# Attention and two mixture layers in one kernel: w2 and the result moved in 4 KB packets, the first blocks of w_in loaded first, products grouped by tiling

## The chip, the cores and the metric

One core of a Trainium2 chip. Its engines are TensorE (PE in the rows, PEld for its weight loads), VectorE (DVE), ScalarE (ACT), GpSimd (POOL) and SyncE (SP), which here issues all DMAs. The metric is the device time of one execution in microseconds, the median of the runs.

## The reference

Attention with a forgetting bias, a layer of squared ReLU, and a soft mixture of 8 experts, one after the other, over 2304 tokens of width 512:

```python
scores = scale * q @ k.T            # 4 batches, 8 heads, 576 positions, head_dim 64
cum = cumsum(maximum(s, 0))
scores = where(causal, -1e9, scores + minimum(-(cum[:, None] - cum[None, :]), 0))
x = softmax(scores) @ v             # heads side by side: 2304 x 512
x = maximum(x @ w_in, 0) ** 2 @ w_out          # 512 -> 2048 -> 512
logits = x @ phi                    # 32 slots: 8 experts x 4
slot_input = softmax(logits, axis=0).T @ x
for e in range(8):
    slot_out[e] = maximum(slot_input[e] @ w1[e], 0) @ w2[e]    # w1 512x1024, w2 1024x512
out = softmax(logits, axis=1) @ slot_out
```

## The kernel before, in words

Every piece of work is a task: a function that issues instructions, with its buffers, a priority and a planned cost for each engine that can do it. `Plan.add` (line 222) makes a task, `Plan.run` (line 248) simulates the five engines with these costs and writes the program out in the order in which it places the tasks. At each step it looks, engine by engine, for the earliest start and takes the first task by priority that can start within WAIT = 100 ns of it (line 303). `FACTOR` scales the planned costs of an engine, `prio` shifts the priority of what is added inside it, and STEP is 1000 priority steps' worth of one stage. The order on every engine, SP's DMAs included, is what this planner made of the numbers.

Attention works on 16 pairs of heads (a batch and two heads) and tiles of 128 query rows. A score tile is a run of products with 64 partitions by 128 columns of weights (L660 q times k in two f16 parts, L663 the causal mask, L665 the bias), the two heads on the two halves of TensorE's rows. The softmax's probabilities, written by L691, are transposed by DMA (L732) and multiplied with v in L791, with 128 by 64 weights. The rows of 128 tokens, as two f16 parts, go into L833: 4 column blocks of w_in (512 columns each) times 12 products with 128 by 128 weights, in two units of 6. The relu and the square (L848 and after) follow; L873 transposes, L890 multiplies with w_out times phi (128 by 32 weights), L918 to L952 keep the running softmax over tokens and add up slot_input in the basis of the 2048 columns. The MoE tiles start once their four pairs are done, so that attention and L833 alternate on TensorE for most of the time. The form of the weights, 64x128, 64x64, 128x64, 128x32, 32x128 or 128x128, is called the tiling below.

w_in and w_out come as 64-bit numbers and are converted to f32 by ACT, DVE and POOL (`f64_load`, `f64_convert`, L496 to L501), then split into f16 parts (L426 and L432 among them; `scaled` can put L426 on ACT, DVE or POOL). `conv_steps` (L1027) keeps up to 6 blocks of 512 KB loading ahead. The forgetting bias starts from s: 8 DMAs (L1043 to L1046) bring it in, each with 16 partitions; L1054 and L1055 make the cumulative sum, and L1059 to L1062 three bf16 rows of it (`cum3`), which L665 needs.

The tail of the kernel begins at L1240. L1249 multiplies with w_out, L1257 transposes, and for each expert `hidden` (L1270, L1276) makes the 1024 hidden values of all 32 slots from w1, and `project` (L1289) multiplies with half of w2's columns and adds into one PSUM bank for each half, `so`. After the last expert `combine(0)` spreads the sum (L1297), splits it into two bf16 parts (L1298 to L1301) and makes 18 tiles of the result (L1308 and L1309), whose columns 0 to 255 are written; then the experts' second halves and `combine(1)` follow for columns 256 to 511. w1 and w2 are loaded in units of 512 KB (`w_unit`, L1172; `w1_load`, L1195, 4 KB in one run of memory; `w2_load`, L1199, 128 partitions by 4 rows by 256 columns, that is 1 KB runs). The loads of all experts' w1 and first halves of w2 come first, the second halves of all last. The result of two tiles goes out as 128 partitions by 2 rows by 256 columns, 256 KB in 1 KB runs; every fifth tile straddles two batches and goes out alone as 2 by 64 rows by 256 columns.

Of the kernel before, what the change touches and what calls it, by code (L numbers as in the profile page):

```python
# [22 lines left out]
N_QK = 2  # L23
Q_AT = 8
# [19 lines left out]
N_OB = 6  # L44
# [41 lines left out]
FACTOR = {"P": 1.0, "V": 1.15, "A": 1.1, "G": 1.3, "D": 1}  # L86
# [112 lines left out]
class Task:  # L199
    def __init__(self, alts, prio):  # L200
        self.alts, self.prio, self.deps, self.succ, self.bufs, self.end, self.gap = alts, prio, set(), [], [], None, 0


class Plan:
# [134 lines left out]
def attention_moe_softmoe(ctx, tc, qk, v, s, w_in, w_out, w_out_t, phi, w1, w2, cst, out):  # L339
# [191 lines left out]
    def wout_conv(raw, c, kd):  # L531
# [108 lines left out]
    def a_scores(P, i):  # L640
# [15 lines left out]
        if i < 4:  # L656
# [9 lines left out]
            add([*qk, sel, mask, cum3, rows_h], pss, P=((5 if plain(P) else 4) * (10 + n / 2.4) + 200, mul))  # L666
            for h, ps in enumerate(pss):
                add([ps], [(m, 2 + h)], V=(60 + 1.04 * n, lambda ps=ps, h=h: nc.vector.reduce_max(out=m.t[:, 2 + h:3 + h], in_=ps.t[:, 0:n], axis=AX.X)))  # L668
        else:
            for ps, c0, c1 in ((pss[0], 0, 512), (pss[1], 512, 576)):  # L670
# [83 lines left out]
    def a_pv(P, i):  # L754
# [17 lines left out]
        else:  # L772
# [12 lines left out]
            ns = (54 if i < 4 else 46) * len(mms) + 90  # L785
# [6 lines left out]
        add(vv + [pt], [x], P=(ns, mul))  # L792
# [31 lines left out]
    def m_h(t, c):  # L824
# [557 lines left out]
```

## Time and profile before

| what | us |
|---|---|
| median of 3 runs | 574.12 |
| lowest, highest | 570.63, 576.21 |
| the profiled execution, its own time | 577.03 |
| its span, from first to last instruction | 575.3 |
| TensorE busy | 503.0 (87%) |
| VectorE busy | 375.3 (65%) |
| ScalarE busy | 329.2 (57%) |
| GpSimd busy | 191.3 (33%) |
| mean granted clock of TensorE | 0.961 of full speed |
| memory read and written | 77.85 MB, 4.72 MB |

The rows further down are of the profiled execution. Times count from the start of its span; "idle before" is the idle time of the engine just before an instruction, with what ended it.

### The profile page before, as it was taken

What the parts mean: (1) busy time and instruction counts of PE and PEld (TensorE: products, weight loads), DVE (VectorE), ACT (ScalarE), POOL (GpSimd) and SP (SyncE); (2) the same over time, 40 slices, a digit from 0 to 9 for tenths busy, and PEclk for the clock granted to TensorE, in tenths of its full rate; (3) what the DMA queues carried; (4) which work ended last, traced back from release to release, by engine and by line L of the source; (5) the groups of instructions that cost most, each with busy time, mean ns of one, the idle gap of its engine ahead of it and who ended that gap; (6) DMA issues with size and microseconds to landing.
All of it is one profiled execution on the core that took longest, in us unless ns stands there. A gap on an engine that the chain in (4) does not pass through costs nothing.

```text
span 575.3 us, 13522 instructions
## 1 busy us (share of the span) xinstructions
PE 503.0 (87%) x5151; PEld 279.2 (49%) x5153; DVE 375.3 (65%) x977; ACT 329.2 (57%) x820; POOL 191.3 (33%) x319
## 2 busy tenths in 40 slices
PE   1268789989999999999999999999989989799771
PEld 1134446556455565554655555555544544345341
DVE  4777988988997988899898766776454231301210
ACT  2866886877776576775665565654555644311132
POOL 3735854662641733363452223311222100000100
PEclk9996789999999999999999999999998999999976
DMA  7986755244555654874664224442888995499985
GB/s 235 385 283 205 254 154 182 86 148 102 127 136 108 131 126 60 139 159 102 127 116 66 52 56 84 79 96 51 232 273 285 322 329 183 155 361 370 349 268 165
DMA packets 122761, 102.72 MB, mean 179 GB/s; under 512 B 81096, under 2 KB 102216, under 8 KB 122696
## 3 DMA queue, kind: packets, MB, share of 16 engines
q1 hardware_dynamic: 122696, 101.86, 62.8%
q8 instruction: 40, 0.66, 0.5%
q14 instruction: 25, 0.20, 0.1%
HBM read 77.85 MB, written 4.72 MB: 144 GB/s over the span
## 4 chain that ended last, share of the span: by engine, by line
PE 61%; DVE 18%; DMA 7%; ACT 4%; issue 3%; POOL 3%; SPq 1%; ACTq 0%; DVEq 0%; POOLq 0%
PE bank L833 26%; DVE sbuf L432 7%; PE bank L791 5%; PE bank L873 5%; PE bank L660 4%; DVE sbuf L668 3%; PE bank L952 3%; PE bank L1270 3%; PE bank L890 2%; DVE sbuf L425 2%; DMA out_dram<-sbuf 2%; POOL sbuf L426 2%; PE bank L675 2%; PE bank L1289 2%; DMA sbuf<-in_w_dram 2%
## 5 line engine op out<-in xcount | busy, mean ns | idle before, releaser
L833 PE MATMUL bank<-sbuf 128*128 128x512 f16 x864 | 206.2, 382 | 2.1 <-DVE sbuf L432 1.4
L833 PEld LDWEIGHTS <-sbuf 128*128 128x128 f16 x864 | 79.4, 98 | 89.7 <-issue 6.7
L443 ACT COPY sbuf<-bank 128x512 f32<-128x512 f32 (+6 forms) x139 | 63.2, 470 | 102.6 <-PE bank L873 37.8
L691 ACT ACTIVATE sbuf<-bank,sbuf 128x512 f32<-128x512 f32 (+4 forms) x160 | 93.1, 586 | 38.8 <-DVE sbuf L685 36.4
L432 DVE SCALAR_TENSOR_TENSOR sbuf<-sbuf 128x512 f16<-128x512 f32 (+5 forms) x149 | 100.8, 703 | 2.6 <-POOL sbuf L426 1.6
L426 POOL TENSOR_SCALAR sbuf<-sbuf 128x512 f16<-128x512 f32 (+9 forms) x97 | 73.6, 764 | 61.8 <-DVE sbuf L714 26.9
L668 DVE TENSOR_REDUCE sbuf<-bank 128x1 f32<-128x128 f32 (+3 forms) x128 | 58.2, 480 | 5.8 <-PE bank L665 5.4
L713 POOL TENSOR_SCALAR sbuf<-sbuf 128x2 f32<-128x2 f32 (+1 forms) x74 | 17.8, 240 | 132.0 <-ACT sbuf L691 92.7
L791 PE MATMUL bank<-sbuf 128*64 128x128 f16 (+4 forms) x1296 | 57.0, 228 | 1.1 <-DMA sbuf<-sbuf 0.6
L444 DVE COPY sbuf<-bank 128x512 f32<-128x512 f32 (+5 forms) x55 | 28.0, 513 | 43.2 <-PE bank L873 18.8
L848 ACT ACTIVATE sbuf<-bank,sbuf 128x512 f32<-128x512 f32 x53 | 36.4, 688 | 34.3 <-PE bank L833 33.6
L499 POOL TENSOR_SCALAR sbuf<-sbuf 128x512 int32<-128x512 uint8 x46 | 34.7, 755 | 61.3 <-DMA sbuf<-in_w_out_dram 32.9
L660 PE MATMUL bank<-sbuf 64*128 64x128 f16 (+7 forms) x352 | 46.2, 363 | 9.2 <-DMA sbuf<-in_qk_dram 8.9
L873 PE MATMUL bank<-sbuf 128*128 128x128 f32 x288 | 44.7, 278 | 1.7 <-ACT sbuf L443 1.2
L501 DVE SCALAR_TENSOR_TENSOR sbuf<-sbuf 128x512 int32<-128x512 int32 x48 | 35.2, 740 | 16.6 <-ACT sbuf L496 9.4
L449 ACT ACTIVATE sbuf<-sbuf 128x512 bf16<-128x512 f32 (+1 forms) x60 | 39.1, 652 | 8.8 <-DMA sbuf<-in_v_dram 4.3
L873 PEld LDWEIGHTS bank<-sbuf 128*128 128x128 f32 x288 | 34.1, 143 | 17.0 <-ACT sbuf L443 2.2
L496 ACT ACTIVATE sbuf<-sbuf 128x512 f32<-128x512 f32 x48 | 31.1, 663 | 17.8 <-DMA sbuf<-in_w_in_dram 10.4
L791 PEld LDWEIGHTS <-sbuf 128*64 128x64 f16 (+1 forms) x1056 | 28.7, 110 | 17.8 <-issue 16.6
L851 ACT ACTIVATE sbuf<-sbuf 128x512 f32<-128x512 f32 x50 | 31.5, 629 | 8.6 <-DVE sbuf L849 7.6
L425 DVE TENSOR_SCALAR sbuf<-sbuf 128x512 f16<-128x512 f32 (+8 forms) x71 | 34.5, 492 | 1.8 <-DMA sbuf<-in_v_dram 0.5
L744 PE MATMUL bank<-sbuf 128*128 128x128 f32 (+1 forms) x100 | 19.4, 313 | 16.9 <-POOL sbuf L426 12.7
(140 smaller groups left out, 675.0 us busy)
## 6 DMA issues: line engine op xcount, KB each, us to landing
sbuf<-in_w_dram SPq DMA_DIRECT2D x48, 512.0 KB, 8.8
sbuf<-in_qk_dram SPq DMA_DIRECT2D x16, 576.0 KB, 5.1
sbuf<-in_w_in_dram SPq DMA_DIRECT2D x16, 512.0 KB, 7.9
sbuf<-in_w_out_t_dram SPq DMA_DIRECT2D x16, 512.0 KB, 4.1
sbuf<-in_w_out_dram SPq DMA_DIRECT2D x16, 512.0 KB, 4.7
sbuf<-in_w_dram SPq DMA_DIRECT2D x32, 256.0 KB, 5.4
sbuf<-in_v_dram SPq DMA_DIRECT2D x28, 256.0 KB, 3.5
out_dram<-sbuf SPq DMA_DIRECT2D x16, 256.0 KB, 5.1
```

The lines of the kernel that those rows point to most:

```text
L425: "V": (130 + 0.52 * n, lambda: nc.vector.tensor_scalar(out=out_(), in0=in_(), scalar1=scale(), scalar2=None, op0=ALU.mult)),
L426: "G": (244 + 0.834 * n, lambda: nc.gpsimd.tensor_scalar(out=out_(), in0=in_(), scalar1=scale(), scalar2=1.0, op0=ALU.mult, op1=ALU.mult)),
L432: alts = {"V": (base + 1.04 * n, lambda: nc.vector.scalar_tensor_tensor(out=out_(), in0=in_(), scalar=scale(), in1=hi(), op0=ALU.mult, op1 ...
L443: "A": (51 + 0.834 * n, lambda: nc.scalar.copy(out=out_(), in_=in_())),
L449: add(r + [junk], w, A=(186 + 0.834 * n, lambda: nc.scalar.activation(out=junk.t[:, 0:n], in_=in_(), func=AF.Abs, accum_out=acc_())))
L660: nc.tensor.matmul(ps.t[:, 0:n], q_(D[h], slice(128 * i, 128 * i + 128)), k_(D[h], slice(0, n)), start=j == 0, stop=False)
L668: add([ps], [(m, 2 + h)], V=(60 + 1.04 * n, lambda ps=ps, h=h: nc.vector.reduce_max(out=m.t[:, 2 + h:3 + h], in_=ps.t[:, 0:n], axis=AX.X)))
L691: ex = lambda t, o, n, ps, h, k: add([nm, sc, ps], [t, (sums, k)], A=(373 + 0.834 * n, lambda: nc.scalar.activation(out=t.t[:, o:o + n], i ...
L791: nc.tensor.matmul(x.t[64 * h:64 * h + 64, c0:c1], lhs, rhs, start=n == 0, stop=n == len(mms) - 1)
L833: nc.tensor.matmul(ps.t, X.t[:, e, kd, :], w[c].t[:, kd, :], start=kd == 0 and e == 0 and w is wh, stop=kd == KD - 1 and e == 1)
L848: add([ps, (sc, b)], [g], A=(571, lambda: nc.scalar.activation(out=g.t, in_=ps.t, func=AF.Relu, scale=sc.t[:, b, c:c + 1])), V=(630, lambd ...
L873: nc.tensor.transpose(ps.t[:, j * 128:(j + 1) * 128], g.t[:, j * 128:(j + 1) * 128], ident)
```

## The change

It has six parts.

1. w2 is loaded with two consecutive rows per partition (`(p k) f -> p (k f)`, k = 2), all 512 columns: 4 KB runs in units of 512 KB (two 2 KB runs in the first, halved units). `hidden` transposes strided columns so that the hidden values stand in the matching order. Each expert's w1 and w2 are loaded one after the other.
2. `project` works on all 512 columns at once, in one bank; `combine` runs once, for two halves of the columns up to `sst`, and its products go into banks of 512 columns. The result goes out as two consecutive rows per partition (4 KB runs, 512 KB), and a tile that straddles two batches as two DMAs of 64 partitions by 2 KB.
3. The first two blocks of w_in are issued right after the constants, ahead of s and qk; later blocks get a priority that is 30 steps back.
4. s comes in two DMAs of 64 partitions, whose DRAM side reads the 16 rows of a head parity 4 times (outermost dimension 4 with step 0), in place of 8 DMAs of 16.
5. The planner: each TensorE task has a tiling; among the tasks that can start within 100 ns of the earliest, one with the tiling of the product before is preferred, if its priority is at most 6 STEPs behind, and 95 ns are planned for a change of tiling. The planned costs of TensorE's tasks are edited throughout.
6. FACTOR of ACT 1.1 to 1.15, of POOL 1.3 to 1.05; DMA's planned cost 1.2 to 1.08; N_OB 6 to 5 (with buffers of twice the size), h1_p 2 to 3 buffers.

```diff
-FACTOR = {"P": 1.0, "V": 1.15, "A": 1.1, "G": 1.3, "D": 1}
+FACTOR = {"P": 1.0, "V": 1.15, "A": 1.15, "G": 1.05, "D": 1}
...
-                        best = first, e, next((s, t) for s, t in options if s <= first + WAIT)
+                        options = [(s, t) for s, t in options if s <= first + WAIT]
+                        if e == "P":
+                            prio = options[0][1].prio + SAME * STEP
+                            options.sort(key=lambda o: o[1].tiling != tiling or o[1].prio > prio)
+                        best = first, e, options[0]
...
+            if e == "P":
+                ns += 0 if task.tiling == tiling else 95
+                tiling = task.tiling
...
-        add(vv + [pt], [x], P=(ns, mul))
+        add(vv + [pt], [x], P=(ns, mul), tiling=(128, 64))
...
-                    raw[j] = blocks[j][0](*blocks[j][2:])
+                    with prio(0.03 if j >= N_AT_ONCE else 0):
+                        raw[j] = blocks[j][0](*blocks[j][2:])
...
+    next(conv)
+    dma(410, lambda: cs.t, lambda: cst, [], [cs])
     for h in range(2):
-        for e in range(4):
-            o = 64 * h + 16 * e
-            dma(60, lambda o=o: s_sb.t[o:o + 16], lambda h=h: bass.AP(tensor=s.tensor, offset=s.offset + h * S, ap=[[2 * S, B * NP], [1, S]]), [], [(s_sb, o)])
-    dma(410, lambda: cs.t, lambda: cst, [], [cs])
+        dma(240, lambda h=h: s_sb.t[64 * h:64 * h + 64], lambda h=h: bass.AP(tensor=s.tensor, offset=s.offset + h * S, ap=[[0, 4], [2 * S, B * NP], [1, S]]), [], [(s_sb, h)])
     qk_load(pairs[0])
-    with prio(5):
-        next(conv)
...
-    def w2_load(e, hf):
-
-        src = w2[e, :, hf * HD:(hf + 1) * HD].rearrange("(a k p) f -> a p k f", k=4, p=128)
-        wt[e, 1, hf] = w_unit(src[0], []) + w_unit(src[1], [])
+    def w2_load(e):
+
+        wt[e, 1] = [u for g in range(4) for u in w_unit(w2[e, 256 * g:256 * g + 256, :].rearrange("(p k) f -> p (k f)", k=2), [])]
...
-                nc.tensor.transpose(ph.t[:, c * 128:(c + 1) * 128], h1.t[:, c * 128:(c + 1) * 128], ident)
+                nc.tensor.transpose(ph.t[:, c * 128:(c + 1) * 128], h1.t.rearrange("p (q c) -> p c q", c=2)[:, c], ident)
...
-                    w = a2[2 * a + g // 2][1]()[:, g % 2 * HD:(g % 2 + 1) * HD]
-                    nc.tensor.matmul(so.t[32 * g:32 * g + 32, 0:HD], z.t[:, 4 * a + g, :], w, start=e == 0 and a == 0, stop=e == E - 1 and a == 1)
+                    nc.tensor.matmul(so.t[32 * g:32 * g + 32, :], z.t[:, 4 * a + g, :], views[4 * a + g][1](), start=e == 0 and a == 0, stop=e == E - 1 and a == 1)
...
-                rows = out[row:row + 128 * n, hf * HD:(hf + 1) * HD].rearrange("(a p) d -> p a d", p=128)
-                dma(365 * n, lambda rows=rows: rows, lambda n=n, o_=o_: o_.t[:, 0:n * HD].rearrange("p (a d) -> p a d", a=n), [o_], [])
+                dma(1500, lambda row=row, n=n: out[row:row + 128 * n, :].rearrange("(p k) d -> p (k d)", k=n), lambda o_=o_: o_.t.rearrange("p k d -> p (k d)"), [o_], [])
             else:
-                rows = out.rearrange("(b r) d -> b r d", r=S)[b0:b + 1, S - 64:S, hf * HD:(hf + 1) * HD]
-                dma(365, lambda rows=rows: rows, lambda o_=o_: o_.t[:, 0:HD], [o_], [])
+                for j, q_ in enumerate((b0, b)):
+                    dma(370, lambda q_=q_: out[q_ * S + S - 64:q_ * S + S, :], lambda j=j, o_=o_: o_.t[64 * j:64 * j + 64, 0, :], [o_], [])
...
-    combine(0)
-    for e in range(E):
-        plan.at += 100
-        project(e, 1)
-    combine(1)
+    combine()
```

Lines of the changed kernel stand 14 to 18 further down in what follows: L660, L663 and L665 are L674, L677 and L679, L791 is L805, L833 is L847, L1289 is L1295.

SP, the first DMAs of the program. Before:

```order
L419 DMA sbuf<-in_cst_dram 128x306
L419 DMA sbuf<-in_s_dram 16x576 x8
L419 DMA sbuf<-in_qk_dram 128x2x576 x2
L419 DMA sbuf<-in_w_in_dram 128x1024 x6
L419 DMA sbuf<-in_v_dram 128x512 x4
```

and now:

```order
L433 DMA sbuf<-in_cst_dram 128x306
L433 DMA sbuf<-in_w_in_dram 128x1024 x2
L433 DMA sbuf<-in_s_dram 64x1x576 x2
L433 DMA sbuf<-in_qk_dram 128x2x576 x2
L433 DMA sbuf<-in_w_in_dram 128x1024 x4
L433 DMA sbuf<-in_v_dram 128x512 x4
```

Two blocks of w_in have moved ahead of s and qk, and s takes two instructions of 64 partitions in place of eight of 16.

TensorE, two thirds through the program, at the end of a score tile of 384 columns (banks 63 and 69 before, 64 and 62 now). Before:

```order
L665 LDWEIGHTS sbuf
L665 MATMUL bank_63<-sbuf 128x384
L665 LDWEIGHTS sbuf
L665 MATMUL bank_69<-sbuf 128x384
L833 LDWEIGHTS sbuf
L833 MATMUL bank_65<-sbuf 128x512
```

and now:

```order
L679 LDWEIGHTS sbuf
L679 MATMUL bank_64<-sbuf 128x384
L679 LDWEIGHTS sbuf
L679 MATMUL bank_62<-sbuf 128x384
L674 LDWEIGHTS sbuf
L674 MATMUL bank_63<-sbuf 128x384
```

Before, L833 with another tiling came behind the score tile; now a second score tile does. Counted over the whole of TensorE's order, neighbours of unlike tiling go from 358 to 275: 83 to 71 up to the 72nd product of L833, 248 to 191 from there to L1240, 27 to 13 in the tail.

SP, the last DMAs of the program. Before (the last two rows stand four times in turn):

```order
L419 DMA sbuf<-in_w_dram 128x1024 x4
L419 DMA sbuf<-in_w_dram 128x4x256 x18
L419 DMA out_dram<-sbuf 128x2x256 x4
L419 DMA out_dram<-sbuf 2x64x256
```

and now, to the end:

```order
L433 DMA sbuf<-in_w_dram 128x512 x10
L433 DMA sbuf<-in_w_dram 128x1024 x29
L433 DMA out_dram<-sbuf 128x1024 x4
L433 DMA out_dram<-sbuf 64x512 x2
L433 DMA out_dram<-sbuf 128x1024 x4
L433 DMA out_dram<-sbuf 64x512 x2
```

The 18 last reads of 512 KB in 1 KB runs are gone, w1 and w2 share one form of 4 KB runs, and the writes are half as many and twice as large.

## Rows read from the trace of the kernel before

**Rows 1.** windows, whole span by stage, columns in the first line

```profile
core 0: us, PE busy (x) PEld busy (x) DVE busy (x) ACT busy (x) POOL busy (x), PEclk, DMA share, GB/s
0.00:8.00 8.00, 0.00 (x0) 0.00 (x0) 1.98 (x3) 1.28 (x1) 4.00 (x18) 1.00 0.47 120
60.00:100.00 40.00, 34.86 (x278) 21.42 (x280) 36.08 (x83) 32.15 (x84) 24.77 (x36) 0.88 0.58 189
100.00:490.00 390.00, 379.96 (x4010) 211.40 (x4007) 284.75 (x742) 243.38 (x594) 132.01 (x215) 1.00 0.57 140
502.00:545.00 43.00, 38.24 (x540) 18.87 (x538) 5.83 (x28) 6.69 (x16) 3.92 (x13) 0.99 1.06 358
545.00:557.00 12.00, 10.00 (x70) 4.57 (x70) 0.60 (x2) 3.08 (x6) 0.12 (x1) 0.60 1.03 340
557.00:561.00 4.00, 2.52 (x23) 2.07 (x23) 1.56 (x4) 1.66 (x4) 0.00 (x0) 1.00 0.24 84
569.00:574.00 5.00, 0.00 (x0) 0.00 (x0) 0.00 (x0) 0.00 (x0) 0.00 (x0) 0.50 0.12 40
```

**Rows 2.** chain that ended last, end of the span (start us, us, what)

```profile
534.96 8.92 DMA sbuf<-in_w_dram
543.92 0.84 PE bank L1289 x8
545.69 7.74 DMA out_dram<-sbuf
```

**Rows 3.** the same chain in the middle, across two changes of tiling

```profile
363.65 0.62 PE bank L791 x18
364.28 1.40 PE bank L833 x6
365.68 0.44 PE bank L873 x4
366.11 1.29 PE bank L833 x6
```

**Rows 4.** windows, three stretches with DMA engines full, columns as in Rows 1

```profile
12.00:17.00 5.00, 1.13 (x10) 0.52 (x6) 3.38 (x12) 4.30 (x15) 3.15 (x6) 1.00 1.02 415
525.00:545.00 20.00, 16.55 (x232) 8.10 (x224) 3.80 (x17) 3.54 (x8) 2.68 (x9) 0.98 1.10 349
549.00:553.00 4.00, 4.00 (x25) 2.46 (x18) 0.00 (x0) 0.96 (x2) 0.00 (x0) 0.50 1.08 363
```

**Rows 5.** timeline, first 13 us (start us, us, engine, line, operation, count, [idle before, releaser])

```profile
1.19 3.65 SPq L419 DMA_DIRECT2D sbuf<-in_s_dram  x8
6.26 0.46 DVE L1054 TENSOR_SCALAR sbuf<-sbuf 128x576 f32<-128x576 f32 x1 [2.99 <-DMA sbuf<-in_s_dram]
11.35 0.29 PE L665 MATMUL bank<-sbuf 64*128 64x128 bf16 x2 [1.50 <-DVE sbuf L1062]
12.47 0.66 ACT L496 ACTIVATE sbuf<-sbuf 128x512 f32<-128x512 f32 x1 [10.45 <-DMA sbuf<-in_w_in_dram]
```

**Rows 6.** timeline, TensorE in the last 25 us, columns as in Rows 5

```profile
552.94 0.42 PE L1308 MATMUL bank<-sbuf 96*128 96x256 bf16 x1
553.15 0.42 PE L1309 MATMUL bank<-sbuf 128*128 128x256 bf16 x1
553.93 1.75 PE L1289 MATMUL bank<-sbuf 128*32 128x256 f32 x24
556.31 0.70 PE L1297 MATMUL bank<-sbuf 128*128 128x256 f32 x2 [0.63 <-DVE sbuf L444]
558.77 0.27 PE L1309 MATMUL bank<-sbuf 128*128 128x256 bf16 x1 [0.95 <-DVE sbuf L1301]
558.88 0.27 PE L1308 MATMUL bank<-sbuf 96*128 96x256 bf16 x1
```

**Rows 7.** POOL's L426, and TensorE's waits for it before 120 us

```profile
L426 POOL TENSOR_SCALAR sbuf<-sbuf 128x512 f16<-128x512 f32 (+9 forms) x97 | 73.6, 764 | 61.8 <-DVE sbuf L714 26.9
PE bank L744 <- POOL sbuf L426: 12.7, 8, 3.9
```

More of the change, by code (lines that the diff above doesn't have):

```diff
@@ L23 @@
 N_QK = 2
+D_COST = 1.08
+N_AT_ONCE = 2
+SAME = 6
 Q_AT = 8
@@ L43 @@
 PR_W = 60
-N_OB = 6
+N_OB = 5
 GR = 15
@@ L201, in __init__ @@
         self.alts, self.prio, self.deps, self.succ, self.bufs, self.end, self.gap = alts, prio, set(), [], [], None, 0
+        self.tiling = None
 class Plan:
@@ L220, in prio, with add @@
         self.at -= int(steps * STEP)
-    def add(self, r=(), w=(), **alts):
+    def add(self, r=(), w=(), tiling=(128, 128), **alts):
         task = Task({e: (FACTOR[e] * ns, f) for e, (ns, f) in alts.items()}, self.at)
+        task.tiling = tiling
         self.at += 1
@@ L254, in run @@
         columns = {}
+        tiling = None
         def pe_time(at, ns):
@@ L1212, in tail @@
         return arena.want(Pool(arena), n, shape, dt, when)
-    h1_p = tail(2, [128, 512], F32, gt_p)
-    s3_p = tail(2, [128, 2, DM // 2], BF16, gt_p)
+    h1_p = tail(3, [128, 512], F32, gt_p)
+    s3_p = tail(1, [128, 2, DM], BF16, gt_p)
     dgt, sit = (tail(1, shape, F32, gt_p).new() for shape in ([128, 4, 4, NS], [128, KD, NS]))
@@ L1224, in attention_moe_softmoe @@
         arena.want(c4_p, 2, [128, 4, 4, NS], BF16, w_p)
-    ob_p = tail(N_OB, [128, 512], F32, w_p)
+    ob_p = tail(N_OB, [128, 2, 512], F32, w_p)
     for e in range(E):
         w1_load(e)
-        w2_load(e, 0)
-    for e in range(E):
-        w2_load(e, 1)
+        w2_load(e)
     chain([], [ssum], [
@@ L1261, in attention_moe_softmoe @@
     NG = FE // 4
-    sos_ = ps_s.new("so"), ps_x0.new("so")
+    so = ps_x0.new("so")
     def hidden(e):
@@ new lines, in project, with combine @@
+            ts = []
+            for t, _ in views[4 * a:4 * a + 4]:
+                if t not in ts:
+                    ts.append(t)
+            add([z, *ts], [so], P=(870, mul), tiling=(128, 32))
+    def combine():
+        sst, w, halves = s3_p.new(), DM // 2, []
+        for h in range(2):
+            o = slice(h * w, h * w + w)
+            sos, p4, r = h1_p.new(), ps_h.new("D"), h1_p.new()
+            evacuate(lambda sos=sos: sos.t[:, 0:w], lambda o=o: so.t[:, o], w, [so], [sos])
+            add([sos, cs], [p4], P=(1.7 * w, lambda sos=sos, p4=p4: nc.tensor.matmul(p4.t[:, 0:w], rep4, sos.t[:, 0:w], start=True, stop=True)))
+            evacuate(lambda o=o: sst.t[:, 0, o], lambda p4=p4: p4.t[:, 0:w], w, [p4], [(sst, h)])
+            add([p4, (sst, h)], [r], V=(70 + w, lambda o=o, p4=p4, r=r: nc.vector.tensor_tensor(out=r.t[:, 0:w], in0=p4.t[:, 0:w], in1=sst.t[:, 0, o], op=ALU.subtract)))
+            add([r], [(sst, 2 + h)], V=(130 + 0.52 * w, lambda o=o, r=r: nc.vector.tensor_copy(out=sst.t[:, 1, o], in_=r.t[:, 0:w])),
+                A=(93 + 0.834 * w, lambda o=o, r=r: nc.scalar.copy(out=sst.t[:, 1, o], in_=r.t[:, 0:w])))
+            add([r], [(sst, 2 + h)], V=(70 + w, lambda o=o, r=r: nc.vector.tensor_tensor(out=sst.t[96:128, 1, o], in0=r.t[96:128, 0:w], in1=sst.t[96:128, 1, o], op=ALU.subtract)))
+            halves.append(o)
@@ L1324, in attention_moe_softmoe @@
         hidden(e)
-        project(e, 0)
+        project(e)
         if CT_LATE and e == E - 2:
@@ L1328, in attention_moe_softmoe @@
                 m_c(t0, nt)
-    combine(0)
-    for e in range(E):
-        plan.at += 100
-        project(e, 1)
-    combine(1)
+    combine()
     with tc.manual_schedule():
```

67 lines of the change are left out of this document (29 added, 38 removed).

## The prediction

> **What bounds the kernel now.** I read the windows over the whole span first, to see which limit holds in which stretch. From 100 to 490 us TensorE is busy 379.96 of 390 us at full clock, 97%, and every other engine has slack [rows 1]. From 502 to 557 us the DMA engines are full (share over 1.0, 340 to 358 GB/s) [rows 1]. From 60 to 100 us VectorE is the fullest engine, 36.08 of 40 us [rows 1]. The last 18 us, from 557 on, move little: 84 GB/s from 557 to 561, 40 GB/s from 569 to 574 with a DMA share of 0.12, which is 2 engines of 16 [rows 1]. Then the chain of waits: at its end stand a read of w2, the product on it and a write of the result [rows 2], so the tail hangs on DMA. In its middle it runs along TensorE: a unit of 6 L833 products takes 1.40 us behind L791, which has another tiling, and 1.29 behind L873, which has the same [rows 3]. Last the start: L665 waits until 11.35 us for the rows made from s, and ACT until 12.47 us for the first block of w_in [rows 5].
>
> The sum is made against the profiled execution, 577.0 us (span 575.3), which lies 2.9 above the median of 574.1; the 2.9 come off at the end.
>
> **The start: -2 us.** SP needs 3.65 us to issue the eight DMAs of s [rows 5], 0.46 each; two cost 0.9, so 2.7 us of issue go. In the first 8 us DMA moves 120 GB/s where it could move 415 [rows 1, 4]: 8 x (1 - 120/415) = 5.7 us of DMA time are unused, and with w_in's 1 MB issued at once perhaps half of that is filled. The first two blocks of w_in (1.05 MB, 2.5 us at 415) should be there at 4 to 5 us instead of 12.47. Against this, s comes later. Its two DMAs have an outermost dimension of 4. The trace shows what a small outermost dimension does: the last writes, 2 by 64 rows by 256 columns, run on 2 engines at 40 GB/s [rows 1]. Four engines would give 80 GB/s, and the 295 KB of s take 3.7 us behind 1 MB of w_in: they land near 8.7 us, not 6.26 [rows 5], and the first scores' bias, 5.1 us later as before (6.26 to 11.35), near 13.8. That is 2.5 us on the path of the first score tile; it is off the path if the conversion of w_in on ACT, POOL and VectorE is what the first 100 us wait for, as VectorE's 36.08 of 40 us suggests [rows 1]. Bounds: -4 (all of the idle DMA time that ACT's 10.45 us of waiting allow) and +2.5 (the late s counts, nothing else does). I take -2, nearer to the gain because VectorE is the bound behind the start.
>
> The Trainium skill, page DMA: Bandwidth & Descriptors, section Why a DMA increments its semaphore by 16 and not by 1, says that the engines of a DMA are the largest number up to 16 that divides the outermost dimensions, which for a leading step of zero with 4 copies is 4. This trace agrees for 2 (share 0.12). By it the sum is as it stands, with s at 8.7 us; were s on all 16 engines, the start would be some 2 us better.
>
> **The grouping by tiling: -5.5 us.** A change of tiling costs 1.40 - 1.29 = 0.11 us [rows 3]. Between the start and the tail 248 - 191 = 57 changes go by the order of the program. 57 x 0.11 = 6.3 us; the planner's own figure, 95 ns, gives 5.4. TensorE is 97% busy there [rows 1], so nearly all of it is on the path; the 12 that go before the 72nd L833 product lie where VectorE is the bound and count nothing, the 14 of the tail lie under the DMA stream and count nothing until that ends. The price of grouping is that a task with worse priority goes first, so something else can come late; attention ends some 40 L833 products later in the order (84 of the 864 are left after the last scores' tiles, 126 before), which cost 0.216 us each by 1.29/6 [rows 3]; 84 of them are 18 us of cover for the last softmax work. Bounds: -7 (more, if the planner's better costs fill waits) and -2 (half the changes fall into waits, and some waits are new). I take -5.5.
>
> **w2 in 4 KB runs: -5 us.** Three stretches with full DMA engines differ by the run: 415 GB/s for w_in's 4 KB runs (12 to 17 us), 349 for w2's 1 KB runs (525 to 545), 363 for the result's 1 KB writes (549 to 553) [rows 4]. The 18 last reads of 512 KB, 9.44 MB, take 27.0 us at 349 and 22.7 at 415: -4.3. In the stretch before, 502 to 525, w1's 4 KB runs mix with w2's 1 KB runs at 358 over all [rows 1]; a third of those 8 MB gains another 1 or so, at most 2. Ahead of 502 the DMA share is 0.57 [rows 1], and the loads wait for buffers, not for the engines: nothing. Bounds: -6.3 (4.3 + 2) and -3 (reads reach only 392 in the mix with the wide products: 9.44/392 = 24.1). I take -5.
>
> The Trainium skill, page DMA: Bandwidth & Descriptors, section Specifications, puts the line rate from 512 B on and the memory's limit for one core near 358 GB/s. The trace does not agree, since 415 stands in it. By that rule this term is nothing and the sum 5 us higher.
>
> **From the last read of w2 to the end: -1.5 us.** Before: in 545 to 557 the engines move 12 x 340 = 4.1 MB [rows 1], of which 2.36 MB are the first half of the result, so 1.7 MB are reads, some 5 us; the last read lands near 551, an estimate, and 24.3 us later the span ends. In these the second half's products begin at 553.93, its sum is spread at 556.31, the first output product with both parts starts at 558.77 [rows 6], and the write stream then carries 2.36 MB, ending on two writes with 2 engines, which take 569 to 574 [rows 1]. Now nothing is written before the last read: all 4.72 MB come after it. Landing 0.5, the last expert's project (8 products of 256 columns took 0.84 [rows 2], of 512 twice that, up to 1.7), the chain from its end to the first bytes of a write (555.7 to 561 before, 5.3 to 5.6 us; with the second half's splitting and a second bank to copy, 7.4), then 4.72 MB at 363 to 415 GB/s, 13.0 to 11.4, and 1.5 for the completion of the last write: 21.7 to 24.1, middle 22.9 against 24.3. The single tiles go as two DMAs of 64 partitions, so the 5 us at 40 GB/s go. What can take it away: TensorE. Its 72 output products ran 0.21 us apart at a granted clock of 0.50 (552.94 and 553.15) and 0.11 apart when the clock was 1.00 (558.77 and 558.88) [rows 4, 6]. 0.50 is the 1.2 GHz level; in 502 to 545, before it fell, the clock was 0.99 and TensorE busy 38.24 of 43 us, and from 545 to 557 its mean is 0.60 [rows 1]. At 0.213 each 72 take 15.3 us, longer than the writes, which adds 2 to 4. Bounds: -5 (415 GB/s, the copies hidden) and +4. I take -1.5.
>
> POOL gets 32 more instructions by the order, VectorE 29 fewer, ACT 18 fewer; N_OB and h1_p cost nothing, since five buffers of twice the size hold more than six did. These are priced under the rivals.
>
> Sum: -2 - 5.5 - 5 - 1.5 = -14.0, so 563.0 for an execution like the profiled one, 560 against the median of 574.1.
>
> **The rivals.** Above or below the forecast:
>
> More is gained (550 us): the planner's truer costs shorten waits in the first 100 us too, where TensorE waits 12.7 us for POOL [rows 7], and each term comes out near its far bound: -4 - 7 - 6.3 - 5 = -22.3, or 552, and 2 more from those waits. For it: those waits are there. Against: VectorE is the bound there. Chance 0.10.
>
> The run length is worth nothing (565): without the 5 us, if the 415 of the early window is w_in's and not the run's. Against it: the reads and the writes of 1 KB show 349 and 363 in two places, the 4 KB reads 415 [rows 4]. Chance 0.08.
>
> The gains cancel (572): s late costs 2.5 where 2 were to be won (+4.5), and the output products at 0.213 us, now all in one run behind a stretch in which TensorE waits for loads, give the +4, so +5.5 on that term; half of the grouping is lost (+2.5): 563 + 12.5 - 2.9 = 572.6. For it: the clock was 0.50 at the same place before. Chance 0.15.
>
> Slower (583): POOL becomes what VectorE and TensorE wait for. FACTOR for POOL falls from 1.3 to 1.05, so the planner believes it faster and gives it 32 more instructions; L426 takes 0.764 us there [rows 7], and TensorE already waits for it 8 times for 12.7 us ahead of 120 us. With 30 of them on the path, 30 x 0.76 = 23 us: 560 + 23 = 583. It decides from 14 us on, that is 18 of the 32 on the path. Against it: POOL is busy 24.77 of 40 us from 60 to 100 [rows 1], so it has room. Chance 0.08.
>
> **How the numbers follow.** The forecast has 0.59; alone its range is 552 to 568, the sum with two of its four terms near one bound. Together with the rivals, 549 to 571 leaves out some 2 in 10: the slower case, most of the case in which gains cancel, a few below. A change of 1% (5.7 us) is about what a measurement of this kernel tells from none, as the three runs are 5.6 us apart. Faster by over 1%, below 568.4: the forecast, more gain, the run length and a little of the cancelling case, 0.76. Within 1%: most of the cancelling case and an edge of the forecast, 0.16. Slower, above 579.9: 0.08.
>
> **What would show it right or wrong.** In the changed profile: ACT's first conversion near 5 us and VectorE's first work on s near 8.7, with a DMA share near 0.25 while s moves alone; the busy share of TensorE from 100 to 490 about as high with that stretch 5 to 6 us shorter; 400 GB/s or more while the last w2 reads run; one write stream of 11 to 13 us to the end without a stretch at 40 GB/s; L1326 and L1327 (the output products) at 0.11 us. The prediction is wrong if TensorE's waits for POOL before 120 us grow well above 12.7 us, if the reads of 4 KB stay at 350 GB/s, or if the output products, not the writes, set the end.

## The result, and the profile after

| | median, us | ratio to before, 95% interval |
|---|---|---|
| before, 20 runs | 575.83 | |
| changed kernel, 20 runs | 567.75 | 0.9891 (0.9862 to 0.9921) |
| changed kernel in a second comparison, beside experiments | 565.84 | 0.9824 (0.9798 to 0.985) |
| in a third | 566.20 | 0.9847 (0.9806 to 0.9889) |
| in a fourth | 566.41 | 0.9859 (0.9827 to 0.9892) |

The change makes the kernel faster by 1.1%, 6.3 us (0.0109 x 575.8); later comparisons give 8 to 10 us. 14.0 were forecast. The ratio compares the runs without three that lie well above the rest (580.40 and 665.47 of before, 973.81 of the changed kernel) and is not that of the medians, which are 8.1 us apart. The intervals of the first and the second comparison don't overlap, and what sets the two apart is not shown. The profiled execution took 565.6 us, span 563.8, against 577.0 and 575.3 before: the two profiles lie 11.4 us apart, more than the medians, since the profiled execution of before was 1.2 us above its median and this one 2.2 below.

The windows of the changed kernel, by stage, answer to [rows 1, 4]:

```profile
core 0: us, PE busy (x) PEld busy (x) DVE busy (x) ACT busy (x) POOL busy (x), PEclk, DMA share, GB/s
0.00:8.00 8.00, 0.00 (x0) 0.00 (x0) 0.94 (x2) 2.52 (x4) 5.21 (x20) 1.00 0.69 202
60.00:100.00 40.00, 32.76 (x219) 18.25 (x220) 36.14 (x83) 30.26 (x76) 30.28 (x40) 0.79 0.61 195
100.00:490.00 390.00, 378.29 (x4074) 216.76 (x4074) 281.83 (x719) 239.13 (x584) 154.45 (x238) 1.00 0.56 140
502.00:525.00 23.00, 22.26 (x276) 10.98 (x279) 1.87 (x11) 2.40 (x7) 1.25 (x4) 0.93 1.03 411
525.00:537.00 12.00, 9.20 (x106) 3.03 (x98) 0.56 (x3) 0.37 (x1) 0.31 (x1) 1.00 1.03 408
540.00:549.00 9.00, 6.86 (x40) 2.93 (x33) 2.89 (x7) 2.45 (x7) 0.00 (x0) 1.00 0.02 10
552.00:562.00 10.00, 3.19 (x28) 2.41 (x25) 2.76 (x4) 2.72 (x5) 0.00 (x0) 0.82 1.01 382
```

From 100 to 490 TensorE is as full as before (378.29 of 390 us, 379.96 before); it holds more products in it. While w1 and w2 are read the DMA engines move 411 and 408 GB/s where w2's 1 KB runs gave 349. From 540 to 549 they move 10 GB/s: this is the chain from the last read to the first write. Then 382 GB/s from 552 to 562, and no stretch with 2 engines.

The chain that ended last, its end (start us, us, what), answers to [rows 2]:

```profile
521.90 10.16 DMA sbuf<-in_w_dram
532.13 10.10 DMA sbuf<-in_w_dram
542.27 1.08 PE bank L1295 x4
549.04 2.65 DMA out_dram<-sbuf
553.28 4.12 DMA out_dram<-sbuf
```

The last read lands at 542.23, the last project follows at 542.27, the first write runs from 549.04. The span ends at 563.8, 21.6 us after the last read; in three more executions of the changed kernel it is 22.5 to 22.8. In the trace of before, the completion signals of the DMAs have the last read, issued at 544.23, land at 552.72, 22.5 us before the end. Two output products of the changed kernel, as in [rows 6]:

```profile
548.08 0.27 PE L1327 MATMUL bank<-sbuf 128*128 128x256 bf16 x1
548.19 0.27 PE L1326 MATMUL bank<-sbuf 96*128 96x256 bf16 x1
```

They start 0.11 us apart: the granted clock was 1.00 from 540 to 549 us, which is the 2.4 GHz level.

The start, as in [rows 5]:

```profile
2.13 1.36 SPq L433 DMA_DIRECT2D sbuf<-in_s_dram  x2
5.92 0.66 ACT L510 ACTIVATE sbuf<-sbuf 128x512 f32<-128x512 f32 x1 [3.90 <-DMA sbuf<-in_w_in_dram]
12.07 0.46 DVE L1066 TENSOR_SCALAR sbuf<-sbuf 128x576 f32<-128x576 f32 x1 [4.69 <-DMA sbuf<-in_s_dram]
13.29 0.80 PE L674 MATMUL bank<-sbuf 64*128 64x128 f32 x4 [13.29 <-DMA sbuf<-in_qk_dram]
18.46 0.29 PE L679 MATMUL bank<-sbuf 64*128 64x128 bf16 x2 [4.21 <-DVE sbuf L1074]
```

The first block of w_in is converted from 5.92 us, not 12.47. But s is worked on from 12.07, not 6.26, and the second group of score products waits 4.21 us, to 18.46, for the rows made from s.

POOL's L440 (L426 before; behind the bar its busy us and mean ns) and TensorE's waits for it before 120 us (us in all, times, longest), as in [rows 7]:

```profile
L440 POOL TENSOR_SCALAR sbuf<-sbuf 128x512 f16<-128x512 f32 (+9 forms) x128 | 95.6, 753 | 63.4 <-DVE sbuf L728 16.7
PE bank L758 <- POOL sbuf L440: 12.8, 9, 3.5
```

128 instructions, 97 before; TensorE waits as long as before, 12.8 us.

Two sums are used below. The loss by changes of tiling in one execution: for each product followed by one of another tiling, the distance between the two starts, less the median distance behind products of the same form when the tiling stays; added up until L1240's work (L1247 in the changed kernel) begins (distances over 0.6 us beyond the median are left out as waits). It was 56.2 us before and 46.1 in the changed kernel. The waits: what the trace's list of TensorE's waits adds up to between 30 us and the same point, 27.1 and 30.5 us. The tail's work began at 501.1 us before, at 495.4 now, and took 74.2 and 68.4 us.

### The profile page after: what moved, and what is told of

Same layout as the page of the kernel before. It is cut to its first block, busy times and chain, and to the rows that moved or that the text cites. A ratio compares the mean times of both kernels' runs of the same rounds, so it can differ in the third digit from the quotient of the medians.

```text
span 563.8 us, 13264 instructions
## 1 busy us (share of the span) xinstructions
PE 494.1 (88%) x5025; PEld 277.9 (49%) x5025; DVE 375.0 (67%) x948; ACT 321.8 (57%) x802; POOL 222.6 (39%) x351
## 5 line engine op out<-in xcount | busy, mean ns | idle before, releaser
L847 PE MATMUL bank<-sbuf 128*128 128x512 f16 x864 | 201.7, 379 | 1.3 <-ACT sbuf L820 0.8
L847 PEld LDWEIGHTS <-sbuf 128*128 128x128 f16 x864 | 81.8, 98 | 88.8 <-issue 4.1
L440 POOL TENSOR_SCALAR sbuf<-sbuf 128x512 f16<-128x512 f32 (+9 forms) x128 | 95.6, 753 | 63.4 <-DVE sbuf L728 16.7
L705 ACT ACTIVATE sbuf<-bank,sbuf 128x512 f32<-128x512 f32 (+4 forms) x160 | 93.4, 589 | 40.6 <-DVE sbuf L699 30.6
L457 ACT COPY sbuf<-bank 128x512 f32<-128x512 f32 (+6 forms) x129 | 59.5, 475 | 98.1 <-PE bank L887 31.6
L446 DVE SCALAR_TENSOR_TENSOR sbuf<-sbuf 128x512 f16<-128x512 f32 (+5 forms) x146 | 105.3, 748 | 9.9 <-POOL sbuf L440 9.1
L674 PE MATMUL bank<-sbuf 64*128 64x128 f16 (+7 forms) x352 | 47.0, 363 | 15.0 <-DMA sbuf<-in_qk_dram 14.1
L862 ACT ACTIVATE sbuf<-bank,sbuf 128x512 f32<-128x512 f32 x56 | 38.4, 686 | 35.2 <-PE bank L847 35.1
L805 PE MATMUL bank<-sbuf 128*64 128x128 f16 (+4 forms) x1296 | 55.1, 228 | 1.5 <-DVE sbuf L446 0.7
L458 DVE COPY sbuf<-bank 128x512 f32<-128x512 f32 (+7 forms) x63 | 32.0, 512 | 31.8 <-PE bank L887 18.3
L887 PE MATMUL bank<-sbuf 128*128 128x128 f32 x288 | 45.4, 280 | 5.1 <-POOL sbuf L864 2.0
L463 ACT ACTIVATE sbuf<-sbuf 128x512 bf16<-128x512 f32 (+1 forms) x60 | 39.0, 651 | 13.2 <-DVE sbuf L515 11.5
L510 ACT ACTIVATE sbuf<-sbuf 128x512 f32<-128x512 f32 x48 | 31.6, 671 | 16.1 <-DMA sbuf<-in_w_out_dram 7.7
L805 PEld LDWEIGHTS <-sbuf 128*64 128x64 f16 (+1 forms) x1056 | 28.8, 110 | 17.4 <-issue 16.4
L758 PE MATMUL bank<-sbuf 128*128 128x128 f32 (+1 forms) x100 | 19.6, 314 | 14.3 <-POOL sbuf L440 13.1
L705 ACT ACTIVATION_READ_ACCUMULATOR sbuf<-bank,sbuf 128x1 f32 x160 | 32.0, 200 | 0.0
L865 ACT ACTIVATE sbuf<-sbuf 128x512 f32<-128x512 f32 x44 | 27.7, 630 | 4.8 <-DVE sbuf L863 3.7
## 6 DMA issues: line engine op xcount, KB each, us to landing
sbuf<-in_w_dram SPq DMA_DIRECT2D x48, 512.0 KB, 10.1
sbuf<-in_w_in_dram SPq DMA_DIRECT2D x16, 512.0 KB, 10.1
```

The costliest lines, as they stand in the source:

```text
L440: "G": (244 + 0.834 * n, lambda: nc.gpsimd.tensor_scalar(out=out_(), in0=in_(), scalar1=scale(), scalar2=1.0, op0=ALU.mult, op1=ALU.mult)),
L446: alts = {"V": (base + 1.04 * n, lambda: nc.vector.scalar_tensor_tensor(out=out_(), in0=in_(), scalar=scale(), in1=hi(), op0=ALU.mult, op1 ...
L457: "A": (51 + 0.834 * n, lambda: nc.scalar.copy(out=out_(), in_=in_())),
L463: add(r + [junk], w, A=(186 + 0.834 * n, lambda: nc.scalar.activation(out=junk.t[:, 0:n], in_=in_(), func=AF.Abs, accum_out=acc_())))
L674: nc.tensor.matmul(ps.t[:, 0:n], q_(D[h], slice(128 * i, 128 * i + 128)), k_(D[h], slice(0, n)), start=j == 0, stop=False)
L705: ex = lambda t, o, n, ps, h, k: add([nm, sc, ps], [t, (sums, k)], A=(373 + 0.834 * n, lambda: nc.scalar.activation(out=t.t[:, o:o + n], i ...
```

## The experiments

**Each part by itself.** The start, the planner and the tail, each alone in the kernel before.

The diffs are parts of the change's own: for the start, the parts 3 and 4 of the list above; for the planner, 5 and 6 without the buffers; for the tail, 1, 2 and the buffers. A line or two of each:

```diff
+    next(conv)
+    dma(410, lambda: cs.t, lambda: cst, [], [cs])
...
+                            options.sort(key=lambda o: o[1].tiling != tiling or o[1].prio > prio)
...
+    def w2_load(e):
```

> The kernel before with the start alone: w_in's first two blocks ahead of s and qk, s in two DMAs of 64 partitions, later w_in blocks set back. Forecast: -2 us against before. Rival (s late): the cumulative sum begins near 12 us as in the changed kernel's trace, 5.8 us later than before, and the time is 2 to 5 us above before's.

> The kernel before with the planner alone (tilings, preference, 95 ns, planned costs, FACTOR). 283 neighbours of unlike tiling for 358. Forecast: -5.5 us. Rival (the reordering makes new waits, POOL above all): -2 to +2, with TensorE's waits for POOL before 120 us above 12.7 us.

> The kernel before with the tail alone: w2 and the result in 4 KB runs, columns undivided. Forecast: -6.5 us (5 from w2's reads, 1.5 from the end). Rival (the gain of before's profile was an execution with a low clock in the tail): -3 to -4, since the usual execution of before has no such stretch.

> The changed kernel once more, for its spread. By the two profiles it should be 11.5 us below before; by the median of 20 runs 6 to 8. If its profile differs from the first by 2 to 4 us, the stage in which it does shows what varies from execution to execution: the clock where TensorE idled, or the DMA stream.

Measured, on one chip: the start 574.13 (0.9993, 0.9968 to 1.0018), the planner 570.72 (0.9927, 0.9899 to 0.9955), the tail 570.23 (0.99, 0.9872 to 0.9928), the whole 565.84. With before at 574.85 that is -0.4, -4.2, -5.7, together -10.3, and -10.1 for the whole: on this chip the three parts add up. The start is worth nothing, neither the 2 us of the forecast nor the loss of 2 to 5 of its rival: the 72nd product of L833 starts at 145.1 us, at 145.2 before. And s is as late as in the changed kernel; the first work on it:

```profile
12.45 0.46 DVE L1058 TENSOR_SCALAR sbuf<-sbuf 128x576 f32<-128x576 f32 x1 [5.02 <-DMA sbuf<-in_s_dram]
```

In the profiles the tail's work took 69.6 us with the tail alone, 72.9 and 72.3 with the start and the planner, which keep the old tail. Before's 74.2 is the longest of the old ones, so part of what was read from it is not in the median. But a low clock there is nothing rare, as the rival of the third expectation would have it: the granted clock was 0.50 from 549 to 553 before [rows 4], 0.50 from 543 to 549 with the start alone and 0.53 from 537 to 544 with the planner alone. From the last read to the end these two took 22.1 and 21.5 us, no more than the changed kernel.

**s by eight DMAs.** The same place in the order, 16 rows outermost.

```diff
-        dma(240, lambda h=h: s_sb.t[64 * h:64 * h + 64], lambda h=h: bass.AP(tensor=s.tensor, offset=s.offset + h * S, ap=[[0, 4], [2 * S, B * NP], [1, S]]), [], [(s_sb, h)])
+        def four(h=h):
+            for e in range(4):
+                o = 64 * h + 16 * e
+                nc.sync.dma_start(out=s_sb.t[o:o + 16], in_=bass.AP(tensor=s.tensor, offset=s.offset + h * S, ap=[[2 * S, B * NP], [1, S]]))
+        add([], [(s_sb, h)], D=(D_COST * 240, four))
```

> The changed kernel beside the next three, as their yardstick: 6 to 10 us below before. If it comes out at 566 again, the first set of 20 runs, in which some lay at 570 to 573, had something these have not.

> The changed kernel, s in eight DMAs of 16 partitions (16 outermost) at the same place of the same order, all else as it was. If the start gained nothing because s came late on 4 engines: the cumulative sum begins near 8 us in place of 12, and the time falls by 2 to 4 us. Rival (VectorE and POOL bind the first 100 us, s's lateness lies beside them): within 1 us of the changed kernel.

566.20 for the changed kernel, 567.63 for this one (0.9866, 0.9833 to 0.9898): no gain. Its timeline:

```profile
2.11 6.21 SPq L1064 DMA_DIRECT2D sbuf<-in_s_dram  x8
9.90 0.46 DVE L1070 TENSOR_SCALAR sbuf<-sbuf 128x576 f32<-128x576 f32 x1 [2.50 <-DMA sbuf<-in_s_dram]
15.46 0.29 PE L679 MATMUL bank<-sbuf 64*128 64x128 bf16 x2 [2.16 <-DVE sbuf L1078]
```

s is there 2.2 us earlier and the score products 3.0 us, with SP issuing for 6.21 us; yet the 72nd product of w_in (L847) starts at 142.9 us, and at 142.2 in the profile of the changed kernel beside it. The lateness of s is not what holds up the first products of w_in.

**The run length of w2.** Every load of w2 in two DMAs: column halves, 1 KB runs; one row of each partition, 2 KB runs; halves of the partitions, 4 KB runs. The order of all else stays. The inner lines of the three in turn (16 loads of half a unit, whose runs are 2 KB already, are split in the same way or, for 2 KB, left):

```diff
-            dma(1460, lambda: t.t.rearrange("p a b -> p (a b)"), lambda: src, r, [t])
+                for h in range(2 if two else 0):
+                    o = slice(256 * h, 256 * h + 256)
+                    nc.sync.dma_start(out=t.t[:, :, o], in_=src.rearrange("p (k f) -> p k f", k=2)[:, :, o])
...
+                    nc.sync.dma_start(out=t.t[:, h], in_=src[:, 512 * h:512 * h + 512])
...
+                    o = slice(64 * h, 64 * h + 64)
+                    nc.sync.dma_start(out=t.t[o].rearrange("p a b -> p (a b)"), in_=src[o])
```

> The changed kernel, each w2 load in two column halves of 1 KB runs, in the same order. If 4 KB runs read at 410 and 1 KB runs at 349 GB/s: the stretch with w2 runs at 370 to 380 over all and the time rises by 4 to 5 us. Rival (the run length is worth nothing): within 1 us.

> The changed kernel, each w2 load as two DMAs of 128 partitions and 2 KB runs, as many DMAs as with 1 KB runs. If the run length sets the rate (1 KB 349, 4 KB 410 GB/s): 1 to 3 us slower than the changed kernel. Rival (the number of DMAs did it): 5 to 7 us slower, as with 1 KB runs.

> The changed kernel, each w2 load as two DMAs of 64 partitions, 4 KB runs kept: as many DMAs as in the kernel with 1 KB runs. If the run length made that one 6 us slower: within 1 us of the changed kernel. Rival (the number of DMAs did it): 5 to 6 us slower.

1 KB: 572.78 (0.9959, 0.9925 to 0.9992), 6.6 us above the changed kernel on its chip. 2 KB: 566.87 (0.9873, 0.9837 to 0.991), 0.5 above it. 64 partitions: 593.82 (1.0315, 1.027 to 1.036), some 26 to 28 us above the changed kernel by the ratios. Windows of the stretch of w2's last reads, in this order, columns as above:

```profile
520.00:550.00 30.00, 23.37 (x212) 7.10 (x204) 1.67 (x9) 1.12 (x3) 1.55 (x5) 0.94 1.07 374
```

```profile
520.00:537.00 17.00, 14.30 (x162) 5.29 (x154) 1.12 (x6) 0.74 (x2) 0.93 (x3) 1.00 1.03 398
```

```profile
520.00:570.00 50.00, 31.55 (x222) 8.70 (x224) 2.52 (x15) 1.80 (x6) 1.56 (x5) 0.82 1.04 272
```

w1 and w2 together run at 374, 398 and 272 GB/s, the changed kernel at 408. Slice by slice (0.5 us each, 520 to 540, the same order) the reads of w1, whole in all three, and those of w2 stand apart, four or so units of each in turn:

```profile
GB/s 410 401 410 424 375 367 361 346 358 344 350 352 340 352 350 365 369 375 393 408 399 426 401 401 410 403 397 358 365 365 338 358 344 348 356 338 352 352 369 389
```

```profile
GB/s 401 397 414 401 418 410 401 418 426 365 373 397 389 385 385 389 389 385 385 385 369 385 401 418 418 410 418 410 410 414 381 397 397 381 389 389 377 385 393 389
```

```profile
GB/s 238 229 262 229 246 205 238 254 238 246 205 229 221 213 295 393 410 401 401 401 442 418 393 238 139 131 205 229 262 229 254 279 205 262 205 270 213 254 229 270
```

The slices near and above 400 GB/s are w1's, as taken from the order of the loads; w2's reads run near 350 with 1 KB runs, near 385 with 2 KB, mostly between 200 and 280 in halves of 64 partitions. Each load of w2 in these stretches is two DMAs in all three. Over the whole kernel w1 and w2 take 120, 104 and 120 DMAs, 80 in the changed kernel: 24 more cost 0.5 us with 2 KB runs, 40 more cost 6.6 with 1 KB. So it is the run of 1 KB that costs, somewhat more than the 4 to 5 us expected, and runs of 2 KB would have done. Halves of 64 partitions were meant as the control for the number of DMAs and can't be it: their time is outside of both expectations, and they have a cost of their own, whose cause is open.

**The preference for the same tiling.**

```diff
-                            options.sort(key=lambda o: o[1].tiling != tiling or o[1].prio > prio)
```

> The changed kernel without the preference for the same tiling (95 ns and the planned costs stay); 373 neighbours of unlike tiling for 275, 68 of the 98 between start and tail. At 0.093 to 0.11 us each on the path: 6.3 to 7.5 us slower. Rival (changes of tiling lie half in waits, or the preference makes waits of its own): 0 to 3 us slower.

579.40 (1.0073, 1.0045 to 1.0102), 13.2 us above the changed kernel beside it. That is more than both expectations. Its loss by changes of tiling is 56.2 us, 10.1 more than 46.1. The sum ends where the tail's work begins; up to there the two traces have 369 and 283 changes, 86 more: 0.12 each, near the price of [rows 3]. The waits are as before (32.1 us, 30.5 and 30.8 in two executions of the changed kernel); the other 3 us are not assigned. In the changed kernel three units of L833 in a row are seen in the chain, at 0.216 each and without a change between them:

```profile
302.03 3.88 PE bank L847 x18
```

**The planned costs.** The changed kernel with FACTOR as before; with TensorE's costs as before (the second edit below stands for all of them); with both, and DMA's, as before.

```diff
-FACTOR = {"P": 1.0, "V": 1.15, "A": 1.15, "G": 1.05, "D": 1}
+FACTOR = {"P": 1.0, "V": 1.15, "A": 1.1, "G": 1.3, "D": 1}
...
-            add([wh[c], wl[c], X], [ps] + ([g] if k0 == 0 else []), P=(644 * H_UNIT, mul))
+            add([wh[c], wl[c], X], [ps] + ([g] if k0 == 0 else []), P=(640 * H_UNIT + 40, mul))
```

> The changed kernel with FACTOR as before (POOL 1.3, ACT 1.1): POOL gets its old share of work, 279 neighbours of unlike tiling for 275. If the 1.05 loads POOL at a cost: 2 to 5 us faster than the changed kernel. Rival (POOL has slack, 44 of 100 us at most behind 100 us): within 1.5 us of it.

> The changed kernel with TensorE's planned costs as before; preference, 95 ns and FACTOR stay; 282 neighbours of unlike tiling. If the edited costs are what made the kernel without preference 13 us slower than the changed one (98 changes of tiling at 0.1 us are only 10): some us faster here. Rival (truer costs plan better): 0 to 3 us slower.

> The changed kernel with all planned costs and factors as before (TensorE's, DMA's, POOL's and ACT's), preference and 95 ns kept; 336 neighbours of unlike tiling, since tasks start less often within 100 ns of each other. 61 more changes at 0.09 to 0.16 us: 5.5 to 9.8 us slower. Rival (it is the planned costs, not the changes of tiling, that set the time): outside of that, on either side.

Old FACTOR: 561.88 (0.9742, 0.9702 to 0.9781). Old TensorE costs: 582.01 (1.011, 1.0072 to 1.0148). All old: 593.00 (1.0297, 1.0264 to 1.0331). To take TensorE's edited costs back costs 14 to 16 us (1.011 against 0.9824 to 0.9859; 0 to 3 were expected): with the old ones the changes of tiling cost no more (45.4 us), but the waits are 40.6 us where 30.5 stand in the changed kernel. With all old, where 5.5 to 9.8 us were expected, the loss by tiling is 55.8 us and the tail's work takes 83.9; that its reads are planned later is likely, but not shown.

What the edits are worth hangs on the others. The kernel without the preference (0.7% above before) and the one with TensorE's old costs (1.1% above) are slower than before, though both hold the tail's part, which by itself takes off 1.0%. So with either one missing, the planner's part costs some 10 to 12 us, and whole it gains 4.2. Even if FACTOR's edit, which is in both and comes next, makes 6.5 to 8.6 us of that, preference and edited costs pay only together here, and 13.2 and 14 to 16 us are not what each would add to the kernel before.

FACTOR's edit goes the wrong way, so it was taken apart:

> The changed kernel as the yardstick of the next two on this chip: 6 to 10 us below before.

> FACTOR as before (POOL 1.3, ACT 1.1), once more. If the edit of FACTOR costs what the chips before suggest: 4 to 6 us faster than the changed kernel, 13 to 15 below before. Rival (the two chips differed): within 1.5 us of the changed kernel.

> The changed kernel with POOL's factor alone back at 1.3 (ACT stays at 1.15), 294 neighbours of unlike tiling for 275. If POOL's 1.05 is what costs: 3 to 6 us faster than the changed kernel. Rival (any other plan is as good or bad by chance, and 19 more changes of tiling cost 2): 0 to 3 us slower.

> The changed kernel with ACT's factor alone back at 1.1 (POOL stays at 1.05), 287 neighbours of unlike tiling for 275. If ACT's 1.15 is what costs: 5 to 7 us faster than the changed kernel, 13 to 15 below before. Rival (a plan is better or worse by the interplay of all its numbers): anything within 3 us of the changed kernel.

> The kernel before with the planner's part but FACTOR as before; 291 neighbours of unlike tiling, 358 before. If the edit of FACTOR costs 6 us in any surrounding: 10 us below before (the planner's part gained 4.2 with it). Rival (it costs only in the changed kernel's plan): 3 to 6 us below before.

On one chip: the changed kernel 566.41; with the old FACTOR 559.09 (0.9746, 0.971 to 0.9782), 6.5 us by the ratios; with POOL's factor alone at 1.3, 567.70 (0.988, 0.9844 to 0.9916). On another: ACT's alone at 1.1, 570.20 (0.9899, 0.9878 to 0.9919); the planner's part with old FACTOR in the kernel before, 562.34 (0.9777, 0.9755 to 0.9799), 8.6 us better than the planner's part with the edit. So the edit costs 6.5 to 8.6 us in either surrounding, and only both factors together undo it: with one of them back, where 3 to 7 us were to be won, the kernel is 1.2 us slower (POOL) and, by the ratios, 2 to 4 (ACT). POOL's L440 and TensorE's waits for it before 120 us, in the changed kernel of that chip:

```profile
L440 POOL TENSOR_SCALAR sbuf<-sbuf 128x512 f16<-128x512 f32 (+9 forms) x128 | 94.6, 745 | 64.0 <-DVE sbuf L728 16.4
PE bank L758 <- POOL sbuf L440: 11.5, 7, 3.3
```

with the old FACTOR:

```profile
L440 POOL TENSOR_SCALAR sbuf<-sbuf 128x512 f16<-128x512 f32 (+9 forms) x107 | 81.5, 766 | 78.4 <-DVE sbuf L728 33.4
PE bank L758 <- POOL sbuf L440: 6.9, 5, 2.4
```

in the kernel with POOL's factor alone at 1.3, in the one with ACT's alone at 1.1, and then in the planner's part with the edit and without it:

```profile
PE bank L758 <- POOL sbuf L440: 6.7, 5, 2.4
```

```profile
PE bank L758 <- POOL sbuf L440: 15.3, 9, 5.0
```

```profile
PE bank L758 <- POOL sbuf L440: 14.3, 8, 4.7
```

```profile
PE bank L758 <- POOL sbuf L440: 8.6, 6, 4.2
```

With the edit POOL gets 128 of the scalings in both surroundings, without it 107 and 113; TensorE waits 11.5 and 14.3 us for them with it, 6.9 and 8.6 without. With ACT's factor alone POOL has 127 and TensorE waits 15.3. With POOL's factor alone the wait is as short, 6.7, but the loss by changes of tiling is 51.4 us (46.1 in the changed kernel; 294 neighbours of unlike tiling for 275), and the one may take the other back. In the planner's part by itself the waits make the difference (all of TensorE's, 29.1 with the edit, 22.5 without, with the tail's work beginning 6.8 us earlier). In the changed kernel they don't add up so: with the old FACTOR the waits for POOL fall by 4.6, others grow (27.2 and 27.7 in all), the loss by tiling falls from 47.0 to 44.7, and the tail's work begins at 488.6 instead of 495.3. Some 4 us of that stay unassigned. But most of what the edit costs is there by 145 us. In the changed kernel, with the edit and then without it:

```profile
0.00:145.00 145.00, 105.07 (x852) 62.47 (x854) 119.88 (x292) 100.25 (x274) 96.33 (x148) 0.94 0.65 208
0.00:145.00 145.00, 103.27 (x925) 63.69 (x926) 121.56 (x318) 109.68 (x297) 84.72 (x137) 0.94 0.69 215
```

Without the edit TensorE has started 925 products by then, 852 with it, at the same clock, and the 72nd product of L847 starts at 139.7 us, not at 144.1; in the planner's part by itself it starts at 141.0, not at 145.6. So 4.4 and 4.6 of the 6.6 and 6.8 us are won where TensorE waits for POOL. Still, a changed order moves the time by some us in any case, as the two runs with one factor show, and two surroundings are few: that the edit costs is measured twice, that it does so through POOL is likely, not shown.

The changed kernel with the old FACTOR is faster than both kernels: 559.09.

## Why the prediction was wrong

The time lies in the range (549 to 571) and the sign was right, but 14.0 us were forecast and 6.3 were measured, 8 to 10 later. Two steps of the sum failed: the start's -2, which gave nothing, and FACTOR, which stood in it at nothing and costs 6.5. By its steps:

- The start, -2: wrong, 0 (0.9993). The step that failed is "nearer to the gain because VectorE is the bound behind the start". w_in's first block did come 6.5 us earlier, and s came not at 8.7 but at 12.07 us. Neither counts: with the start alone the 72nd product of L833 comes no earlier (145.1 us, 145.2 before), and s in eight DMAs gave nothing. That fits VectorE as the bound, busy 36.14 of 40 us from 60 to 100 as before (36.08), and then an earlier w_in had nothing to gain either. The late s was forecast as moving alone, with a DMA share near 0.25; it did not, the share was 0.79 from 6 to 8 us and 1.06 from 8 to 10, so this trace does not tell how many engines carried it.
- The tiling, -5.5: the planner's part, FACTOR included, gave 4.2. That changes of tiling cost is right, and the price nearly so. Without the preference the changed kernel is 13.2 us slower, and its loss by tiling is 10.1 us more, 0.12 for each change. Between before and after the loss fell by 10.1 us too, for 69 changes less (57 and the 12 of the start), 0.15 each: the median of the kind in [rows 3], 128x64 to 128x128, is 0.15 over the whole trace, from 128x32 to 128x128 it is 0.20 and from 64x128 to 128x128 0.22 to 0.25. What was left as a bound is the line "more, if the planner's better costs fill waits": with TensorE's old costs, preference kept, the kernel is slower than before.
- FACTOR, costed at nothing: this step took most of the forecast away. The prediction named the mechanism as its slower rival (POOL believed faster, given 32 more instructions, TensorE waiting for it) and priced it at 23 us for 30 instructions on the path, or nothing. It measured 6.5 us in the changed kernel and 8.6 in the planner's part, and was in the sum at 0, because POOL "has room". It has (30.28 of 40 us busy from 60 to 100), and the edit costs all the same. With the old FACTOR the kernel lies 14.6 us (0.0254 x 574.9) below before, near the sum's 14.0, but that is luck: the start gave nothing, and the planner's part with the old FACTOR gave 12.8 (0.0223 x 575.7) where 5.5 stood. The sign to look for was given, "TensorE's waits for POOL before 120 us grow well above 12.7", and was the wrong one: they stayed at 12.8, while without the edit they are 6.9. A cost can hide in a number that stays.
- w2's reads, -5: right. 408 to 411 GB/s against 349, and 6.6 us for 1 KB runs put back; from the begin of the tail's work to the last read 46.8 us where before took 51.7. The Trainium skill (page DMA: Bandwidth & Descriptors, section Specifications) puts the line rate from 512 B on. The runs here don't agree for 1 KB (near 350 GB/s where 4 KB give 408), and nearly do for 2 KB (near 385).
- The end, -1.5: nothing to tell. The 24.3 us of before rest on a last read near 551, an estimate; the trace has it land at 552.72, so 22.5 us against 21.6, and other executions lie at 21.4 to 22.8 with either tail. Of the terms the landing took 0.04 us for 0.5, the chain from the last project to the first write 5.7 for 7.4, the writes with their completion 14.8 for 12.9 to 14.5. The output products ran 0.11 us apart, not 0.213. Both tail terms together were forecast at -6.5 and measured -5.7. That the last 18 us of before "move little" is misread for 561 to 569, which move 267 GB/s; no term rests on it.
- The reference: the profile of before, 577.0, has a tail of 74.2 us, 1.3 and 1.9 more than the two others with the old tail. The sum took its 2.9 us off at the end, but the terms were still read from it.

## What to carry to other kernels

When a planner's numbers are edited together, give each edit a term in the sum and try the kernel without it: here a bad factor (6.5 us) went along unseen in a part that gained 4.2. What an edit is worth in one plan need not be its worth in another: the preference and the edited costs each made the kernel slower than before without the other. A wait that stays the same in a profile may be one that should have fallen. A transfer put first gains only what waits for it in the end: work on w_in from 5.92 us instead of 12.47 did not make its 72nd product come earlier.

## What the hardware showed unexpectedly

Loads of w2 in halves of 64 partitions, with 4 KB runs, moved 272 GB/s with w1's loads between them where 128 partitions moved 398 with as many DMAs to a load and 2 KB runs; the DMA share was 1.04, so the engines were held, not idle. With w1's loads between them, runs of 2 KB read as fast as 4 KB within 3% (398 and 408 GB/s); by themselves they read near 385.
